# A fused linear-attention and gated-MLP kernel: q's features from narrow products spread by way of DRAM, low weight parts last in one block, all step orders replanned

## The chip, the cores and the metric

The kernel runs on one core of one Trainium2 chip. A core has TensorE (matrix products into PSUM), VectorE, ScalarE, GpSimd and SyncE, which run side by side and wait for one another by semaphores; SyncE issues the DMAs here. The metric is the device time of one execution in microseconds.

## The reference

Four batches, four heads of 32 features, 1088 positions. First a linear attention whose feature map is an outer product, then a gated MLP with a spatial product over the positions:

```
phi(x) = (S1 x) outer (S2 x)            # 8 x 8 = 64 features of each head
kv  = sum_s phi(k) v ;  z = sum_s phi(k)
x   = phi(q) kv / (phi(q) z + 1e-6)     # heads side by side: [4, 1088, 128]
h   = gelu(x @ w_in)                    # 1024 wide; u, v = its two halves
v_n = layernorm(v) * g_ln
v_s = w_sg @ v_n + b_sg                 # over the 1088 positions
out = x + (u * v_s) @ w_out
```

Everything is float32.

## The kernel before, in words

Positions lie in nine tiles of 128 (t; the last has 64) or in three thirds of 364, 362 and 362 columns (ci). The 512 wide hidden half is cut into four blocks of 128 (db).

Outside batch 0's first stretch every product is made of rounded parts (fp32r): a high part, and a low part that is the remainder, so that one f32 product is three of them: high x high, high x low, low x high. The spatial product (`Gate.spatial`, L326 to 336) adds these three for each t and ci, so a block is 3 x 26 products. Its weights' low parts, w_l, are made on VectorE in the head (`w_lo`, L919 to 925), one subtraction of 128x1088 for each t.

The **head** is batch 0's attention and its block 0, with f32 operands (L911: `pz<-w_f,vn`), built by the class Head. Its work is a set of steps with an engine, a length, a list of steps before it, and a tail; `Steps.order` (L509) plans them by due times that it reckons backwards (`far`), and the program is written out in that order. Loads are steps of SyncE's queue. v is normalised tile by tile: statistics, then a reciprocal root for a group of tiles (`GROUPS`; `norm`, L622, its last part on GpSimd, L634 to 645; for the third group VectorE does it all, L275 to 298), then ScalarE writes vn (L303).

Behind the head, `Gate.main` (L406) runs the blocks of each batch. In batch 0 it begins with block 1, all three thirds in one loop over t. Outside the head the order of issue isn't the order of the loops alone: what is ready goes first, within priorities (AHEAD), and in this block the whole first third is issued before the others. The next batch's attention is interleaved with it: the class Side gives each of its steps a time from a table of numbers, FIRST for batch 1 and LATER for the others, and `tick` issues what is due after each piece of spatial work.

In that attention (`Attention`, L123 to 240), k's features are a product with both factors' columns side by side (`k1`, L136), a copy and a multiplication (L143), summed with v into pkv (`k2`, L157). q's features go by six parts (third x half of the features). `load_q` loads q twice, `q1` makes a rounded copy on 64 partitions and its remainder on the others (L186, L187), and `q2` computes each of the two factors already spread to all features (L195, L196), copies one (L200), multiplies (L203), rounds (L206) and takes the remainder on GpSimd (L208):

```
for i in range(2):
    pp = bank(f"pab{self.b}_{j}_{i}")[:, :cw]
    mm(pp, lhsT=sab_h[:, i], rhs=self.qt[j][:, :cw], start=True, stop=False)
    mm(pp, lhsT=sab_l[:, i], rhs=self.qt[j][:, :cw], start=False, stop=True)
```

`q3` (L210) multiplies the features with kv (numerator and denominator, pnd) and divides (L231).

Of the kernel before, what the change touches and what calls it, by code (L numbers as in the profile page):

```python
# [18 lines left out]
P = 128  # L19
NT = 9  # L20
# [11 lines left out]
GROUPS = ((0, 3), (3, 3), (6, 3))  # L32
# [10 lines left out]
]  # L43
LATER = [
# [22 lines left out]
def tile_kernel(ctx: ExitStack, tc: tile.TileContext, qd, kd, vd, sd, wd, bd, wind, gd, woutd, identd, outd):  # L67
# [5 lines left out]
    cpool = ctx.enter_context(tc.tile_pool(name="const", bufs=1))  # L73
    psum = ctx.enter_context(tc.tile_pool(name="ps", bufs=3, space=PSUM))
# [17 lines left out]
    mask2 = const([P, 2], "mask2")  # L92
    mask4 = const([P, H], "mask4")
    for m, n in ((mask2, 2), (mask4, H)):
        V.memset(m, 0.0)
        for r in range(H):
            V.memset(m[32 * r : 32 * r + 32, r % n : r % n + 1], 1.0)

    mask = const([P, 64], "mask")
    G.memset(mask, 0.0)  # L100
    G.memset(mask[0:64, 0:32], 1.0)
    G.memset(mask[64:128, 32:64], 1.0)
# [3 lines left out]
    sk = const([P, 2, 64], "sk")  # L106
    G.memset(sk[:, 1], 0.0)
    sab_h = const([P, 2, P], "sab_h", F32R)
    sab_l = const([P, 2, P], "sab_l", F32R)
# [11 lines left out]
    for i in range(WARM):  # L121
        mm(bank("warm")[:64, :64], lhsT=mask, rhs=mask, start=True, stop=True)
    class Attention:  # L123
        def __init__(self, b, pool, x):
            self.b, self.pool, self.x = b, pool, x
            self.kp, self.q, self.qt, self.qp = {}, {}, {}, {}
# [7 lines left out]
        def k1(self, t):  # L134
            pk = bank(f"pk{self.b}_{t}")[:, :P]
            mm(pk, lhsT=self.k[:, P * t : P * t + P], rhs=sk.rearrange("p a c -> p (a c)"), start=True, stop=True)  # L136
            yield
            ab = pk[:, 0:64].rearrange("p (h x r) -> p h x r", h=H, x=2)
            kb = self.pool([P, H, R], "kb", f"kb{self.b}_{t}")
            A.copy(kb, ab[:, :, 1])  # L140
            yield
            self.kp[t] = kp = self.pool([P, H, R, R], "kp", f"kp{self.b}_{t}")
            V.tensor_tensor(  # L143
                kp,
                ab[:, :, 0].unsqueeze(3).broadcast_to([P, H, R, R]),
                kb.unsqueeze(2).broadcast_to([P, H, R, R]),
                op=ALU.mult,
            )

        def k2(self, t):  # L150
            kp = self.kp.pop(t).rearrange("p h i j -> p (h i j)")
# [23 lines left out]
        def load_q(self, j):  # L175
            ci, p = divmod(j, 2)
            c0, cw = CH[ci]
            self.q[j] = q = self.pool([P, CW], "qld", f"q{self.b}_{j}")
            for r in range(2):
                load(q[64 * r : 64 * r + 64, :cw], qd[self.b, 64 * p : 64 * p + 64, c0 : c0 + cw])  # L180

        def q1(self, j):
            q, cw = self.q.pop(j), CH[j // 2][1]

            self.qt[j] = qt = self.pool([P, CW], "qt", f"qt{self.b}_{j}", F32R)
            V.tensor_copy(qt[:, :cw], q[:, :cw])  # L186
            V.tensor_sub(qt[64:128, :cw], q[64:128, :cw], f32(qt[64:128, :cw]))  # L187

        def q2(self, j):
            ci, p = divmod(j, 2)  # L190
            cw = CH[ci][1]
            pab = []
            for i in range(2):
                pp = bank(f"pab{self.b}_{j}_{i}")[:, :cw]
                mm(pp, lhsT=sab_h[:, i], rhs=self.qt[j][:, :cw], start=True, stop=False)  # L195
                mm(pp, lhsT=sab_l[:, i], rhs=self.qt[j][:, :cw], start=False, stop=True)  # L196
                pab.append(pp)
            yield
            a = self.pool([P, 512], "r", f"a{self.b}_{j}")[:, :cw]
            A.copy(a, pab[0])  # L200
            yield
            qp = self.pool([P, 512], "r", f"qp{self.b}_{j}")[:, :cw]
            V.tensor_mul(qp, pab[1], a)  # L203
# [857 lines left out]
```

## Time and profile before

| | |
|---|---|
| time, median of 3 runs | 368.19 us (367.65 to 368.26) |
| profiled execution: its time | 367.63 us |
| profiled execution: span | 365.9 us |
| TensorE busy | 353.1 us, 97% |
| VectorE busy | 261.8 us, 72% |
| ScalarE busy | 163.8 us, 45% |
| GpSimd busy | 29.4 us, 8% |
| moved by DMA | 18.47 MB |
| granted TensorE clock, mean | 0.993 |

PE is TensorE, DVE VectorE, ACT ScalarE, POOL GpSimd, SP SyncE. The span runs from the first to the last instruction of the profiled execution, and a little of the execution's time lies around it. Matrix products overlap, so a row's duration is longer than the distance from its start to the next one's. The granted clock is TensorE's share of its full speed.

### The profile page before, as it was taken

What the parts mean: (1) busy time and instruction counts of PE and PEld (TensorE: products, weight loads), DVE (VectorE), ACT (ScalarE), POOL (GpSimd) and SP (SyncE); (2) the same over time, 40 slices, a digit from 0 to 9 for tenths busy, and PEclk for the clock granted to TensorE, in tenths of its full rate; (3) what the DMA queues carried; (4) which work ended last, traced back from release to release, by engine and by line L of the source; (5) the groups of instructions that cost most, each with busy time, mean ns of one, the idle gap of its engine ahead of it and who ended that gap; (6) DMA issues with size and microseconds to landing.
All of it is one profiled execution on the core that took longest, in us unless ns stands there. A gap on an engine that the chain in (4) does not pass through costs nothing.

```text
span 365.9 us, 5574 instructions
## 1 busy us (share of the span) xinstructions
PE 353.1 (97%) x2067; PEld 331.1 (91%) x2067; DVE 261.8 (72%) x626; ACT 163.8 (45%) x355; POOL 29.4 (8%) x60
## 2 busy tenths in 40 slices
PE   8995998999999999999999999999999999999995
PEld 8784657999988999999989999999999999999994
DVE  5786899889799775799897565698888453633234
ACT  5465951254463672445533931435533941331120
POOL 4006001010220000211200000202200000000000
PEclk9998999999999999999999999999999999999999
DMA  7992000150100000511000000100000000100001
GB/s 237 408 396 95 1 2 0 32 161 22 41 20 22 21 2 21 172 41 41 23 21 2 0 2 20 41 32 12 3 0 2 0 0 22 41 2 0 2 0 62
DMA packets 9772, 18.47 MB, mean 50 GB/s; under 512 B 1680, under 2 KB 6672, under 8 KB 9744
## 3 DMA queue, kind: packets, MB, share of 16 engines
q1 hardware_dynamic: 9744, 18.11, 14.5%
q8 instruction: 16, 0.26, 0.3%
q14 instruction: 12, 0.10, 0.1%
HBM read 15.88 MB, written 2.23 MB: 49 GB/s over the span
## 4 chain that ended last, share of the span: by engine, by line
PE 67%; DVE 11%; ACT 2%; issue 2%; DMA 1%; SPq 0%; DVEq 0%
PE pz L331 14%; PE pz L333 14%; PE pz L332 14%; PE pkv L157 3%; PE pu L345 2%; PE pu L347 2%; PE pu L346 2%; PE po L394 2%; PE po L395 2%; PE po L396 2%; PE pz L336 2%; PE pz L335 2%; PE pv L256 2%; PE pv L257 1%; PE pv L255 1%
## 5 line engine op out<-in xcount | busy, mean ns | idle before, releaser
L331 PE MATMUL pz<-w_h,vh 128*128 128x364 f32 (+1 forms) x360 | 119.5, 332 | 0.0
L333 PE MATMUL pz<-w_l,vh 128*128 128x364 f32 (+1 forms) x360 | 118.3, 328 | 0.7 <-DVE w_l L925 0.7
L332 PE MATMUL pz<-w_h,vl 128*128 128x364 f32 (+1 forms) x360 | 118.2, 328 | 0.0
L333 PEld LDWEIGHTS pz<-w_l,vh 128*128 128x128 f32 x360 | 67.6, 188 | 1.2 <-DVE w_l L925 1.0
L331 PEld LDWEIGHTS pz<-w_h,vh 128*128 128x128 f32 x360 | 67.8, 188 | 0.8 <-DVE gt L357 0.3
L332 PEld LDWEIGHTS pz<-w_h,vl 128*128 128x128 f32 x360 | 67.7, 188 | 0.7
L370 ACT CAST gh<-gt 128x362 fp32r<-128x362 f32 (+1 forms) x47 | 23.2, 495 | 86.2 <-PE po L395 80.2
L357 DVE SCALAR_TENSOR_TENSOR gt<-pz,g_col,b_bc 128x362 f32<-128x362 f32 (+1 forms) x48 | 28.0, 589 | 38.7 <-PE pz L336 38.3
L208 POOL TENSOR_TENSOR qpl<-qp,qph 128x362 fp32r<-128x362 f32 (+1 forms) x18 | 18.4, 1021 | 182.9 <-ACT kb L140 104.2
L303 ACT ACTIVATE vn<-vn,nm,rs 128x512 f32<-128x512 f32 x36 | 27.6, 809 | 10.0 <-DVE nm L298 7.3
L371 DVE TENSOR_TENSOR gl<-gt,gh 128x362 fp32r<-128x362 f32 (+1 forms) x47 | 25.8, 551 | 5.1 <-ACT gh L370 4.8
L321 DVE TENSOR_TENSOR vl<-vn,vh 128x384 fp32r<-128x384 f32 (+2 forms) x60 | 22.9, 419 | 8.2 <-ACT vh L316 8.1
L350 ACT ACTIVATE u<-pu 128x362 f32<-128x362 f32 (+1 forms) x48 | 22.4, 470 | 12.1 <-PE pu L347 11.8
L365 DVE TENSOR_TENSOR gt<-gt,u 128x362 f32<-128x362 f32 (+1 forms) x48 | 26.8, 560 | 0.4 <-ACT u L350 0.3
L227 DVE RECIPROCAL den<-den 128x362 f32<-128x362 f32 (+1 forms) x9 | 21.7, 2414 | 3.0 <-ACT den L224 2.9
L316 ACT CAST vh<-vn 128x384 fp32r<-128x384 f32 (+1 forms) x63 | 23.5, 419 | 0.9 <-PE pz L336 0.8
L911 PE MATMUL pz<-w_f,vn 128*128 128x362 f32 (+3 forms) x54 | 18.2, 489 | 4.0 <-ACT vn L303 4.0
L260 ACT ACTIVATE vn<-pv 128x512 f32<-128x512 f32 x27 | 15.7, 596 | 12.3 <-PE pv L257 12.2
L263 DVE BATCH_NORM_STATS2 st<-vn 128x6 f32<-128x512 f32 x27 | 18.3, 687 | 3.5 <-ACT vn L260 3.4
L911 PEld LDWEIGHTS pz<-w_f,vn 128*128 128x128 f32 (+1 forms) x54 | 10.1, 194 | 10.9 <-ACT vn L303 4.2
L345 PE MATMUL pu<-x_h,win_h 128*128 128x362 f32 (+1 forms) x48 | 16.7, 348 | 1.1 <-DVE x L231 0.7
L347 PE MATMUL pu<-x_l,win_h 128*128 128x362 f32 (+1 forms) x48 | 15.8, 329 | 0.0
(180 smaller groups left out, 602.9 us busy)
## 6 DMA issues: line engine op xcount, KB each, us to landing
w_f<-in_w SPq DMA_DIRECT2D x9, 544.0 KB, 9.0
vx<-in_v SPq DMA_DIRECT2D x8, 288.0 KB, 4.6
q<-in_q SPq DMA_DIRECT2D x24, 90.5 KB, 2.4
k<-in_k SPq DMA_DIRECT2D x3, 576.0 KB, 4.2
out<-o SPq DMA_DIRECT2D x8, 181.0 KB, 1.9
q<-in_q SPq DMA_DIRECT2D x12, 91.0 KB, 2.4
win_raw<-in_w_in SPq DMA_DIRECT2D x2, 512.0 KB, 7.1
out<-o SPq DMA_DIRECT2D x4, 182.0 KB, 1.8
```

Of the source, the lines that this page charges most:

```text
L303: A.activation(self.vn[:, t], self.vn[:, t], AF.Identity, bias=self.nm[:, t : t + 1], scale=self.rs[:, t : t + 1])
L316: A.copy(vh[:, ts], vs[:, ts])
L331: mm(z, lhsT=vh[:, t], rhs=w_h[:, t, cs], start=(t == 0), stop=False)
L332: mm(z, lhsT=vl[:, t], rhs=w_h[:, t, cs], start=False, stop=False)
L333: mm(z, lhsT=vh[:, t], rhs=w_l[t][:, cs], start=False, stop=False)
L345: mm(pu, lhsT=win_h[:, ws], rhs=xh[:, cs], start=True, stop=False)
L347: mm(pu, lhsT=win_h[:, ws], rhs=xl[:, cs], start=False, stop=True)
L357: V.scalar_tensor_tensor(gt, z, g_col[:, db : db + 1], b_bc[:, c0 : c0 + cw], op0=ALU.mult, op1=ALU.add)
L365: V.tensor_mul(gt, gt, u)
L370: A.copy(gh, gt)
L371: V.tensor_sub(gl, gt, f32(gh))
L911: return mm(zs[ci], lhsT=g.vn[r, t, :P], rhs=w_f[t][r, c0 : c0 + cw], start=(t == 0), stop=(t == NT - 1),)
```

## The change

1. q's features in batches 1 to 3. q is loaded once per third. The two factors are computed narrow, 64 wide, by one set of three products per third (`q2`), copied to SBUF, and spread to the features' partitions by three writes to a buffer in DRAM and two reads back (`spread`). The multiplication (`qp2`) then has both operands in SBUF. k's features are laid out in the same new order (`features`). The eight GpSimd steps that built sab_h and sab_l in the head fall away, and a mask comes with the identity's load.
2. Block 1 of batch 0: all high products first (`spatial_h`), then the 27 with the weights' low parts (`spatial_l`). The steps that make the low parts are due later in the head (tail −10).
3. The head is replanned: a table HEAD is added to the due times, the ends of the loads are modelled in sequence, GROUPS is (0,2)(2,3)(5,4) and only its second group has its norm on GpSimd; q1 and q2 are loaded ahead of v; one half of w_in is loaded behind all of w.
4. FIRST and LATER have new numbers.

```
-GROUPS = ((0, 3), (3, 3), (6, 3))
+GROUPS = ((0, 2), (2, 3), (5, 4))
...
 FIRST = [
-    -16.769, 0.232, -0.448, 2.644, -3.941, 2.17, -14.543, -2.337, 7.458, 11.494, 4.424, -3.889, 5.58, 19.523,
...
+    8.367, 12.087, 9.623, 6.432, 6.419, 24.648, 11.799, 24.091, 14.517, 39.473, 17.629, 25.126, 22.662, 41.732,
...
+    def spread(pool, ab, cw, name):
+        d = dram.tile([2, 2, P, 3 * P], F32, tag="e", name=name + "d", bufs=3)
+        load(
+            d[0].rearrange("p (x j) c -> (p x) j c", j=R)[:, :, :cw],
+            ab[:32, :cw].unsqueeze(1).broadcast_to([32, R, cw]),
+        )
+        for p in range(2):
+            load(
+                d[1, p].rearrange("(i x) c -> x i c", i=R)[:, :, :cw],
+                ab[32 + 16 * p : 48 + 16 * p, :cw].unsqueeze(1).broadcast_to([16, R, cw]),
+            )
+        e = [pool([P, 2, 3 * P], "e" + x, name + x) for x in "ab"]
+        for i in range(2):
+            load(e[i][:, :, :cw], d[i].rearrange("p q c -> q p c")[:, :, :cw])
+        return e
...
+        def q1(self, ci):
+            q, cw = self.q.pop(ci), CH[ci][1]
+            self.qt[ci] = qh, ql = [self.pool([P, CW], "qt", f"qt{self.b}_{ci}{i}", F32R) for i in "hl"]
+            A.copy(qh[:, :cw], q[:, :cw])
+            V.tensor_sub(ql[:, :cw], q[:, :cw], f32(qh[:, :cw]))
...
+            mm(pp, lhsT=sk_h, rhs=qh[:, :cw], start=True, stop=False)
+            mm(pp, lhsT=sk_l, rhs=qh[:, :cw], start=False, stop=False)
+            mm(pp, lhsT=sk_h, rhs=ql[:, :cw], start=False, stop=True)
+            ab = self.pool([64, 3 * P], "ab", f"ab{self.b}_{ci}")
+            A.copy(ab[:, :cw], pp[:64])
+            self.e[ci] = spread(self.pool, ab, cw, f"e{self.b}_{ci}")
+
+        def qp2(self, j):
...
+            a, b = (x[:, p, :cw] for x in self.e[ci])
+            V.tensor_mul(a, a, b)
...
-                for t in range(NT):
-                    if t in (3, 5, 7):
-                        run(self.split(2, 3 * (t // 2 - 1), 3))
+                for i in range(2 * NT):
+                    t = i % NT
+                    if i in (SPL):
+                        run(self.split(2, 3 * SPL.index(i), 3))
                     for ci in range(len(CH)):
-                        self.spatial(zs[ci], 1, ci, t)
+                        (self.spatial_l if i >= NT else self.spatial_h)(zs[ci], 1, ci, t)
...
-                if t0 < 6:
+                if t0 == 2:
                     self.norm(t0, n_)
...
-side = Pool(sp, 1, r=8, kp=3, kb=2, qld=1, qt=3, st=2, vh=2, vl=2, ve=3, y=3, h=3, p=3)
+side = Pool(sp, 1, r=6, kp=3, kb=2, qld=1, qt=3, ab=2, ea=2, eb=2, st=2, vh=2, vl=2, ve=3, y=3, h=3, p=3)
```

Three places of the new order. The first is TensorE around the first spatial product of the head; pv is x times w_in's v half, pz the spatial product, px a transpose of x. Before:

```order
L880 MATMUL pv0_5_427<-win_h_91,x0_h_131 128x512
L881 MATMUL pv0_5_427<-win_l_92,x0_h_131 128x512
L882 MATMUL pv0_5_427<-win_h_91,x0_l_132 128x512
L852 MATMUL px0_2_447<-ident_141,xt0_2_417 128x128 x3
L911 MATMUL pz0_0_0_467<-w_f0_204,vn0_133 128x364
L880 MATMUL pv0_7_484<-win_h_91,x0_h_131 128x512
L881 MATMUL pv0_7_484<-win_l_92,x0_h_131 128x512
```

And in the changed kernel:

```order
L913 MATMUL pv0_5_397<-win_h_84,x0_h_124 128x512
...
L820 MATMUL pab0_5_0_402<-q0_2_140,sab_144 128x384
L820 MATMUL pab0_5_1_404<-q0_2_140,sab_144 128x384
L944 MATMUL pz0_0_0_414<-w_f0_184,vn0_126 128x364
L944 MATMUL pz0_0_1_417<-w_f0_184,vn0_126 128x362
L944 MATMUL pz0_0_2_424<-w_f0_184,vn0_126 128x362
L859 MATMUL pnd0_2_443<-kvx_143,qp0_0_141 128x66
...
L944 MATMUL pz0_0_0_414<-w_f1_193,vn0_126 128x364
...
L885 MATMUL px0_2_463<-ident_73,xt0_2_457 128x128 x3
L944 MATMUL pz0_0_2_424<-w_f1_193,vn0_126 128x362
...
L913 MATMUL pv0_8_475<-win_h_84,x0_h_124 128x512
```

The third transpose and the last products of v now stand behind the first spatial products instead of ahead of them, and two tiles of vn are enough to begin.

The second place is TensorE in block 1 of batch 0 (vh, vl: the parts of v; w_h, w_l: of the weights; pab: q's factors). Before:

```order
L331 MATMUL pz0_1_0_638<-w_h_87,vh0_1_526 128x364
L332 MATMUL pz0_1_0_638<-w_h_87,vl0_1_527 128x364
L333 MATMUL pz0_1_0_638<-w_l7_606,vh0_1_526 128x364
L335 MATMUL pz0_1_0_638<-w_h_87,vh0_1_526 128x364
L136 MATMUL pk1_2_656<-sk_83,k1_628 128x128
L157 MATMUL pkv1_668<-vx_81,kp1_0_648 128x128 x2
L336 MATMUL pz0_1_0_638<-w_l8_608,vh0_1_526 128x364
L136 MATMUL pk1_1_662<-sk_83,k1_628 128x128
L331 MATMUL pz0_1_2_640<-w_h_87,vh0_1_526 128x362
L332 MATMUL pz0_1_2_640<-w_h_87,vl0_1_527 128x362
```

In the changed kernel, where the high products end and the low ones begin:

```order
L363 MATMUL pz0_1_0_618<-w_h_80,vh0_1_479 128x364
L363 MATMUL pz0_1_1_619<-w_h_80,vh0_1_479 128x362
L363 MATMUL pz0_1_2_620<-w_h_80,vh0_1_479 128x362
L226 MATMUL pab1_1_687<-qt1_1h_683,sk_h_78 128x362
L227 MATMUL pab1_1_687<-qt1_1h_683,sk_l_79 128x362
L371 MATMUL pz0_1_0_618<-w_l0_537,vh0_1_479 128x364
L178 MATMUL pk1_1_705<-sk_76,k1_608 128x128
...
L371 MATMUL pz0_1_0_618<-w_l1_574,vh0_1_479 128x364
...
L228 MATMUL pab1_1_687<-qt1_1l_684,sk_h_78 128x362
L371 MATMUL pz0_1_0_618<-w_l3_579,vh0_1_479 128x364
```

No product of the block takes a low weight part before all high ones are issued.

The third place is VectorE, where the low parts are made (kp: k's features; gt: a scaled spatial result; qt: q's remainder). Before:

```order
L925 TENSOR_TENSOR w_l3_594<-w_f3_232,w_h_87 128x1088
L321 TENSOR_TENSOR vl0_1_527<-vn0_133,vh0_1_526 128x384
L925 TENSOR_TENSOR w_l4_598<-w_f4_242,w_h_87 128x1088
L925 TENSOR_TENSOR w_l5_600<-w_f5_250,w_h_87 128x1088
L925 TENSOR_TENSOR w_l6_602<-w_f6_256,w_h_87 128x1088
L321 TENSOR_TENSOR vl0_1_527<-vn0_133,vh0_1_526 128x256
L324 TENSOR_TENSOR vh0_1_526<-vn0_133,vh0_1_526 64x128
L925 TENSOR_TENSOR w_l7_606<-w_f7_260,w_h_87 128x1088
L143 TENSOR_TENSOR kp1_0_648<-pk1_0_644,kb1_0_646 128x256
```

In the changed kernel:

```order
L958 TENSOR_TENSOR w_l2_576<-w_f2_198,w_h_80 128x1088
L666 TENSOR_TENSOR wout_l_87<-wot_551,woe_562 128x512
L958 TENSOR_TENSOR w_l3_579<-w_f3_208,w_h_80 128x1088
L392 SCALAR_TENSOR_TENSOR gt0_0_0_600<-pz0_0_0_414,g_col_88,b_bc_89 128x364
...
L958 TENSOR_TENSOR w_l4_581<-w_f4_216,w_h_80 128x1088
L141 TENSOR_TENSOR kp1_2_647<-pk1_2_643,kb1_2_645 128x256
L958 TENSOR_TENSOR w_l5_583<-w_f5_220,w_h_80 128x1088
L141 TENSOR_TENSOR kp1_0_661<-pk1_0_657,kb1_0_659 128x256
L958 TENSOR_TENSOR w_l6_585<-w_f6_225,w_h_80 128x1088
L220 TENSOR_TENSOR qt1_1l_684<-q1_1_681,qt1_1h_683 128x362
...
L141 TENSOR_TENSOR kp1_1_709<-pk1_1_705,kb1_1_707 128x256
L958 TENSOR_TENSOR w_l8_589<-w_f8_237,w_h_80 64x1088
```

The low parts are spread out between scalings, k features and q steps, which stand ahead of the last ones now.

## Rows read from the trace of the kernel before

**Rows 1.** the page: busy time of each engine; the chain of waits by engine

```profile
PE 353.1 (97%) x2067; PEld 331.1 (91%) x2067; DVE 261.8 (72%) x626; ACT 163.8 (45%) x355; POOL 29.4 (8%) x60
...
PE 67%; DVE 11%; ACT 2%; issue 2%; DMA 1%; SPq 0%; DVEq 0%
```

**Rows 2.** timeline of PE, 59 to 65: start us, us, what [idle before <-releaser]

```profile
60.12 0.43 PE L333 MATMUL pz<-w_l,vh 128*128 128x364 f32 x1 [0.72 <-DVE w_l L925]
...
61.73 0.41 PE L336 MATMUL pz<-w_l,vh 128*128 128x364 f32 x1 [0.34 <-DVE w_l L925]
62.58 0.49 PE L136 MATMUL pk<-sk,k 128*128 128x128 f32 x2 [0.44 <-DVE kp L143]
...
63.07 0.33 PE L332 MATMUL pz<-w_h,vl 128*128 128x362 f32 x1
...
64.89 0.49 PE L331 MATMUL pz<-w_h,vh 128*128 128x362 f32 x2
```

**Rows 3.** stretches: window, us, busy PE, PEld, DVE, ACT, POOL, clock, DMA, GB/s

```profile
10.00:15.00 5.00, 5.00 (x30) 3.81 (x29) 3.58 (x11) 1.19 (x3) 0.00 (x0) 1.00 1.02 413
30.00:35.00 5.00, 1.42 (x3) 0.88 (x4) 4.00 (x12) 2.28 (x4) 4.01 (x14) 0.81 0.03 12
63.00:150.00 87.00, 86.23 (x526) 81.86 (x525) 70.06 (x168) 41.75 (x100) 7.52 (x8) 1.00 0.15 43
150.00:360.00 210.00, 209.30 (x1259) 206.19 (x1257) 138.40 (x322) 87.74 (x192) 10.85 (x11) 1.00 0.06 18
```

**Rows 4.** timeline of PE, 28 to 54, columns as in rows 2

```profile
33.59 1.58 PE L911 MATMUL pz<-w_f,vn 128*128 128x364 f32 x2 [4.05 <-ACT vn L303]
...
36.59 0.39 PE L881 MATMUL pv<-win_l,x_h 128*128 128x512 f32 x1
...
39.58 14.77 PE L911 MATMUL pz<-w_f,vn 128*128 128x362 f32 x46
```

**Rows 5.** groups by line: count | busy us, mean ns | idle before <-releaser

```profile
L195 PE MATMUL pab<-qt,sab_h 128*128 128x362 f32 (+1 forms) x36 | 12.3, 342 | 0.0
...
L925 DVE TENSOR_TENSOR w_l<-w_f,w_h 128x1088 fp32r<-128x1088 f32 (+1 forms) x9 | 11.6, 1289 | 0.4
...
L187 DVE TENSOR_TENSOR qt<-q,qt 64x362 fp32r<-64x362 f32 (+1 forms) x18 | 10.3, 572 | 0.6
...
L186 DVE CAST qt<-q 128x362 fp32r<-128x362 f32 (+1 forms) x18 | 7.0, 389 | 6.5 <-DMA q<-in_q 4.5 <-PE pab L196 1.9
```

**Rows 6.** the page, DMA issues: count, KB each, us from issue to landing

```profile
w_f<-in_w SPq DMA_DIRECT2D x9, 544.0 KB, 9.0
...
k<-in_k SPq DMA_DIRECT2D x3, 576.0 KB, 4.2
out<-o SPq DMA_DIRECT2D x8, 181.0 KB, 1.9
```

**Rows 7.** timeline of POOL, the first group's norm: its first and last step

```profile
28.65 0.19 POOL L634 TENSOR_TENSOR nh<-ny 128x3 f32<-128x3 f32 x1 [21.77 <-DVE ny L631]
...
32.49 0.19 POOL L645 TENSOR_TENSOR nm<-np,rs 128x3 f32<-128x3 f32 x1
```

**Rows 8.** timeline of DVE: the last group's norm, then what follows to block 1

```profile
40.92 0.16 DVE L275 TENSOR_SCALAR ve<-mv 128x3 f32<-128x3 f32 x1
...
43.18 0.68 DVE L620 TENSOR_TENSOR win_l<-wi0t,wi0e 128x512 fp32r<-128x512 f32 x1
...
61.51 0.68 DVE L620 TENSOR_TENSOR wout_l<-wot,woe 128x512 fp32r<-128x512 f32 x1
```

**Rows 9.** views of lines 203 and 365: duration ns min/median/max, first and last start

```profile
L203 DVE TENSOR_TENSOR qp<-pab,a x18: 527/535/539, 71.5 to 260.4; 128x362 f32<-128x362 f32 x12, 128x364 f32<-128x364 f32 x6
...
L365 DVE TENSOR_TENSOR gt<-gt,u x48: 474/530/1306, 64.8 to 360.0; 128x362 f32<-128x362 f32 x32, 128x364 f32<-128x364 f32 x16
```

**Rows 10.** timelines of POOL and DVE at 165, columns as in rows 2

```profile
165.13 1.35 POOL L208 TENSOR_TENSOR qpl<-qp,qph 128x362 fp32r<-128x362 f32 x1 [0.40 <-ACT qph L206]
...
165.57 1.31 DVE L365 TENSOR_TENSOR gt<-gt,u 128x362 f32<-128x362 f32 x1
```

More of the change, by code (lines that the diff above doesn't have):

```diff
@@ L135, in k1 @@
             pk = bank(f"pk{self.b}_{t}")[:, :P]
[L136 removed]
+            mm(pk, lhsT=self.k[:, P * t : P * t + P], rhs=sk, start=True, stop=True)
             yield
[L138 to L140 removed]
+            kb = self.pool([P, 32], "kb", f"kb{self.b}_{t}")
+            A.copy(kb, pk[:, 32:64])
             yield
[L142 to L148, printed above, removed]
+            self.kp[t] = kp = self.pool([P, 2 * P], "kp", f"kp{self.b}_{t}")
+            features(kp, pk, kb)
         def k2(self, t):
[L151 removed]
+            kp = self.kp.pop(t)
             if t == 0:
@@ L173, in kv, with load_q @@
             V.tensor_sub(self.kvs[1], kv, f32(self.kvs[0]))
-        def load_q(self, j):
-            ci, p = divmod(j, 2)
+        def load_q(self, ci):
             c0, cw = CH[ci]
[L178 to L187, printed above, removed]
@@ L210, in q3 @@
+            G.tensor_sub(qpl, a, f32(qph))
         def q3(self, ci):
@@ L329, in spatial, with spatial_l @@
             cs = slice(c0, c0 + cw)
+            last = mm(z, lhsT=vh[:, t], rhs=w_h[:, t, cs], start=(t == 0), stop=False)
             if t < NT - 1:
-                mm(z, lhsT=vh[:, t], rhs=w_h[:, t, cs], start=(t == 0), stop=False)
-                mm(z, lhsT=vl[:, t], rhs=w_h[:, t, cs], start=False, stop=False)
-                mm(z, lhsT=vh[:, t], rhs=w_l[t][:, cs], start=False, stop=False)
-            else:
-                mm(z, lhsT=vh[:, t], rhs=w_h[:, t, cs], start=False, stop=False)
-                mm(z, lhsT=vh[:, t], rhs=w_l[t][:, cs], start=False, stop=True)
+                last = mm(z, lhsT=vl[:, t], rhs=w_h[:, t, cs], start=False, stop=False)
+            return last
+        def spatial_l(self, z, db, ci, t):
+            c0, cw = CH[ci]
+            mm(z, lhsT=self.parts[db][0][:, t], rhs=w_l[t][:, c0 : c0 + cw], start=False, stop=(t == NT - 1))
         def unit(self, pool, db, ci):
@@ L518, in far @@
                     s = steps[n]
-                    way[n] = s[1] + s[6] + max([far(u) for u in users[n]] + [s[7]])
+                    way[n] = s[1] + max(s[6], 0.0) + max([far(u) for u in users[n]] + [s[7]])
                 return way[n]
+            for n, more in zip(steps, HEAD):
+                far(n)
+                way[n] += more
             for n in steps:
                 far(n)
-            free, end, holds, given = {}, {}, {}, {}
+            free, end, holds, given, moved = {}, {}, {}, {}, 0.0
             left, out, rank = set(steps), [], {n: i for i, n in enumerate(steps)}
@@ L551, in order @@
                 free[eng] = t + length
-                end[n] = t + length + late
+                if late < 0:
+                    moved = max(moved, t + length + 1.5) - late / 360
+                    end[n] = moved + 0.4
+                else:
+                    end[n] = t + length + late
                 for b, tag, _ in takes:
@@ L575, in __init__, with load @@
             self.s = Steps()
-            self.dma = 0
-        def load(self, name, kb, f, after=(), queue="SP"):
-            self.dma += kb
-            self.s.at(name, queue, 0.47 if queue == "SP" else 0.1, f, after, late=2.0 + max(0.0, self.dma / 360 - 1.5))
+        def load(self, name, kb, f, after=()):
+            self.s.at(name, "SP", 0.47, f, after, late=-kb)
         def split64(self, name, hi, lo, raw, n, whole, after, late):
@@ new lines, in build, with expand @@
+            at("skh", "A", 0.2, lambda: A.copy(sk_h, sk), ["sk"], late=0.1, tail=-8)
+            at("skl", "V", 0.2, lambda: V.tensor_sub(sk_l, sk, f32(sk_h)), ["skh"], tail=-8)
+            sab = stage([P, 2, 2, P], "sab", "sab")
+            def expand(x, h):
+                part = s[:, R * x : R * x + R].unsqueeze(2 - x).broadcast_to([P, R, R])
+                o = sab[:, x, h // 2].rearrange("q (i h j) -> q h i j", i=R, h=2)[:, h % 2]
+                A.activation(o, part, AF.Copy, scale=mask4[:, h : h + 1])
@@ L732, in build @@
+            for h in range(H):
+                for x in range(2):
+                    at(("sab", x, h), "A", 0.25, lambda x=x, h=h: expand(x, h), [("s", "whole")])
             pk = {}
```

192 lines of the change are left out of this document (87 added, 105 removed), and 35 rows, old and new, of tables (FIRST, HEAD, LATER).

## The prediction

> **What bounds the kernel now.** I read the page first, then a table of stretches, then the idle times of the engine that turned out to matter. On the page TensorE is busy 353.1 of 365.9 us and holds two thirds of the chain that ended last; VectorE comes second with 261.8 [rows 1]. Most of TensorE's instructions behind the head are products of 362 or 364 columns, and they run back to back: between the start at 63.07 and that at 64.89 lie eleven of them, so one more or less costs 1.82 / 11 = 0.165 us, half of the 0.33 us that a row prints as its duration, since neighbours overlap [rows 2]. The stretches show where TensorE stands still. From 63 to 360 us it is idle 0.8 + 0.7 = 1.5 us in all; VectorE is busy 70.1 of the first 87 us there and 138.4 of the other 210 [rows 3]. So behind 63 us the kernel is as long as its list of products, and only fewer products can help. Before that TensorE stands twice. In batch 0's head it waits 4.05 us until 33.59, for ScalarE's normalised v (vn), and then runs at a lower clock: the granted clock from 30 to 35 is 0.81 on average, part of it at the lower level of 1.2 GHz after an idle engine, where the later stretches have 1.00 (2.4 GHz), and the six products that start from 33.59 on need 3.0 us to 36.59 where the same ones at the full clock take four at 0.23 and two at 0.30, 1.5 us. That stop costs 4.05 + 1.5 = 5.6 us [rows 3, 4]. In block 1 of batch 0 three products wait 0.72, 0.34 and 0.44 us for low weight parts and a k feature out of VectorE; from start to start they lose 0.88, 0.51 and 0.68, 2.1 us [rows 2].
>
> The sum below is made against the profiled execution: span 365.9, its own time 367.63, so 1.7 lie around the span. The median of the three runs, 368.19, is 0.56 above it.
>
> **q's features: −7.4.** For each of six parts of a batch and each of two factors a pair of products (L195 and L196, 36 of each in three batches, 72) [rows 5] gives way to three products per third, 27. Every one has 362 or 364 columns, so 45 x 0.165 = 7.4 us go from an engine without slack. VectorE loses 18 casts (7.0) and 18 subtractions (10.3) and gets 9 subtractions of the same length on twice the partitions (9 x 0.57 = 5.1); its 18 multiplications stay, but read two buffers in SBUF instead of PSUM and SBUF. That is 12 us less on an engine that isn't the bound, so nothing by itself. ScalarE swaps 18 copies for 9 casts and 9 copies of equal width: nothing, at 45% busy [rows 1]. GpSimd keeps its 18 subtractions.
>
> What the change adds is the way round DRAM: copy (0.5), three writes, two reads, multiplication (0.54), cast (0.5), GpSimd's subtraction (1.0). A write and a read are both 745 KB in two directions; the nearest rows for one such transfer are 1.9 us for 181 KB and 4.2 us for 576 KB [rows 6]. With some 0.5 us for each issue the chain lasts 0.5 + 1.5 + (1.9 to 4.2) + 1.0 + (1.9 to 4.2) + 0.5 + 0.5 + 1.0 = 9 to 13 us. I take 13, because every row goes to many partitions. In the new order at least 121 TensorE rows, 20 us, lie between a third's products and the first that reads its features. I cost it at nothing: what hides it are those 20 us. If that cover were gone, each third would stop TensorE by what is left of 13. SyncE's queue holds the reads behind the writes, and the next q, k and v loads behind the reads; these are taken up tens of us later, and the queue moved 43 GB/s in 63 to 150 where the early loads ran at 413 [rows 3]. In the queue the wait for the writes is thus long but bare.
>
> **The head: −1.8.** The norm of the first tiles moves from GpSimd to VectorE and covers two tiles instead of three. On GpSimd it lasted from 28.65 to 32.68 [rows 7], 4.0 us, behind VectorE's first three steps; the same twelve small steps on VectorE lasted from 40.92 to 43.18, 2.3 us [rows 8]. I stepped the new order by hand with the mean duration of each instruction. TensorE then runs out of work near 29.0 and gets the first spatial product at 30.3, so 1.3 us idle for 4.05, too short, I take it, to lose the clock. What is late next: v's second half has 384 KB of q1 and q2 put ahead of it, at 413 GB/s [rows 3] 0.9 us, and the products that take it wait for it; 0.35 before the first numerator; and 1.3 around the last third's transpose, since that third comes later and nothing is left to put before it. Together 0.9 + 0.35 + 1.3 + 1.3 = 3.85 new against 5.6 old: −1.8, and the f32 block ends near 52.5 instead of 54.3 [rows 4]. The bounds: −5.6 if none of these waits comes true, and +1.7 if they are half as long again (5.8) and one drops the clock as before (1.5). The value lies near the upper end, because the waits that go are replaced by waits of the same kind.
>
> **Low weight parts last: −1.3.** The block's 51 high products now run before its 27 low ones. TensorE begins them near 53, and reaches the last low one after 51 x 0.165 = 8.4, two small k products (0.4), six q products (1.0), 24 low ones (4.0) and three k products (0.7): 52.5 + 0.5 + 14.5 = 67.5. VectorE had 18.3 us of work from the end of its norm (43.18) to the last low part (61.51) [rows 8]. The new order puts into that stretch three steps of win (1.5), wout's low part (0.6), two k features (0.7), two q subtractions (1.0) and three scalings (1.5): 23.6. Its norm ends near 43.7, so the last part is there at 67.3. Nothing is left to wait for, with 0.2 to spare; a low part (1.29 on VectorE [rows 5]) more would already show. The 2.1 us go, and some 0.8 come back right behind, where the k features that were put off are waited for by their products until about 74. The bounds are −2.1 (nothing comes back) and +2.5 (VectorE two low parts late, 2.6, on top of what is there today).
>
> **The rest: +0.4.** Tables for batches 1 to 3 are new, and somewhere a product will stand. What is idle there today is 1.5 [rows 3], so −1.5 at best; +4 if the first stage's VectorE (81% busy) [rows 3] makes its consumers wait at a few places. I take a value near zero, since VectorE has 12 us less to do.
>
> **Sum:** −7.4 − 1.8 − 1.3 + 0.4 = −10.1: a span of 355.8, 357.5 for such an execution, **358.1** beside the median.
>
> **The rivals.**
> *Better (B).* The head's new waits don't come, nor those behind it. For it: each of my four waits is a difference of sums of mean durations and not longer than their error. Against it: v's second half really arrives later. −7.4 − 5.6 − 1.3 = −14.3, 353.9.
> *Part given back (C).* The stretch from 63 to 150 becomes bound by VectorE, and its share of the gain, 15 x 0.165 = 2.5, is lost; and the head's stop lasts long enough to lose the clock again, 1.5. For it: 81% busy there, with the scalings and k features pushed behind the low parts. Against it: 4 us less of q work per batch. −10.1 + 4.0 = −6.1, 362.1.
> *Slower (D).* GpSimd holds up VectorE. The 18 multiplications took 527 to 539 ns whatever else ran while one operand came from PSUM; the gate's multiplication, two operands in SBUF, took 530 mostly, but 1306 at most [rows 9], and that one, at 165.57, lies under GpSimd's subtraction of 165.13 [rows 10]. If all 18 go from the one kind to the other under such a subtraction, each gains 0.78 us, 14.0 us. They decide from the point where 13 of them lie on TensorE's path (13 x 0.78 = 10.1); with all, 372.1. Against it: the two multiplications of a third stand apart in the order, and a third's features have 7 us to spare. The Trainium skill, "SBUF — State Buffer", section "Who interferes with whom", states that a VectorE instruction with two inputs in SBUF contends with a GpSimd instruction that reads SBUF, and that the other blocks entirely; the two rows agree, 1306 against 530. By that rule alone the gain would be lost; by the slack it is not.
> *No change (E).* Each way through DRAM takes what the loads of w took, 9.0 us for 544 KB [rows 6]. The chain is then 0.5 + 1.5 + 9.0 + 1.0 + 9.0 + 2.0 = 23 us against 20, and each of the tightest thirds, one per batch, stops TensorE 3 us: 9 us in three batches, 367.1, and with the clock lost once more 368.6. It decides only from a transfer of 7.5 us on. Against it: the loads of w queued at 413 GB/s behind one another, and the later stretch moves a tenth of that.
>
> **How the numbers follow.** My forecast has 0.62, B 0.15, C 0.16, D 0.04, E 0.03. The range reaches from B to C with what the bounds of the head and of the rest add, 353.5 to 363.5; D and E and the far ends stay outside. A measurement of this kernel can tell about 0.2% from no change. Forecast, B and C lie on the fast side by more: 0.93; E is within: 0.03; D slower: 0.04.
>
> **What would show it.** The changed profile should have 27 products for q's narrow factors in place of the 72; TensorE busy near 345; one stop of 1 to 2 us before the first spatial product, with a granted clock near 1.00 from 30 to 35; no wait for low weight parts; from 63 to 360 under 3 us idle; the multiplications of the q features partly at 1.3 us. I am wrong in the main if TensorE is idle over 5 us behind 63 us, if a numerator's product waits for q's features, or if the head still loses its clock.

## The result, and the profile after

The changed kernel takes 363.17 us (median of 4 runs, 362.88 to 363.34) against 367.93 for the kernel before; the ratio is 0.987 (95% interval 0.9852 to 0.9887), 4.8 us less. The forecast was 358.1, in a range from 353.5 to 363.5: the sign was right, the median lies just inside the range, and the gain is less than half of the 10.1 us that the sum had. The profiled execution took 363.20, its span is 361.4.

The page of the changed kernel, busy time and chain, as in [rows 1]:

```profile
PE 350.6 (97%) x2022; PEld 321.6 (89%) x2022; DVE 249.3 (69%) x603; ACT 162.4 (45%) x355; POOL 22.0 (6%) x37
...
PE 81%; DVE 9%; ACT 5%; DMA 1%; issue 1%; SPq 1%; POOL 1%; DVEq 0%; ACTq 0%
```

The 45 products are gone, and VectorE is down by the 12 us that were reckoned. TensorE is "97% busy" as it was, but its busy time fell by 2.5 us only. The stretches of the changed kernel, columns as in [rows 3]:

```profile
30.00:35.00 5.00, 4.84 (x24) 3.48 (x25) 4.20 (x14) 3.66 (x6) 2.66 (x12) 1.00 0.04 14
63.00:150.00 87.00, 85.60 (x517) 80.05 (x517) 69.52 (x158) 43.61 (x107) 7.01 (x7) 1.00 0.41 109
150.00:355.00 205.00, 204.53 (x1203) 196.64 (x1201) 126.98 (x305) 83.11 (x184) 11.58 (x12) 1.00 0.18 47
```

The head keeps its clock (1.00 for 0.81). Behind 63 us TensorE is idle 1.4 + 0.5 = 1.9 us, hardly more than before. Its timeline shows the waits in the head and one behind block 1, as in [rows 2, 4]:

```profile
8.43 0.46 PE L788 MATMUL pkv<-vx,vn 128*128 128x128 f32 x2 [0.69 <-DMA vx<-in_v]
9.08 3.17 PE L788 MATMUL pkv<-vx,vn 128*128 128x128 f32 x26 [0.18 <-DMA vx<-in_v]
...
30.16 2.10 PE L944 MATMUL pz<-w_f,vn 128*128 128x364 f32 x6 [1.23 <-ACT vn L335]
...
37.32 0.50 PE L913 MATMUL pv<-win_h,x_h 128*128 128x512 f32 x1 [0.19 <-ACT x_h L888]
...
44.88 7.78 PE L944 MATMUL pz<-w_f,vn 128*128 128x364 f32 x24 [0.19 <-ACT vn L335]
...
69.15 0.60 PE L193 MATMUL pkv<-vx,kp 128*128 128x128 f32 x3 [0.35 <-DVE gt L392]
```

Where the time went is seen by stages. I take a batch's start as the start of the first spatial product of its block 0, and count products in the trace. A stage's length comes from one profiled execution; in two runs of near copies of the changed kernel its third line is 230.10 and 229.80:

| stage | before | changed | difference | forecast |
|---|---|---|---|---|
| head, to its last f32 product | 53.88 | 52.20 | −1.7 | −1.8 |
| batch 0, from block 1 on | 73.28 | 69.82 | −3.5 | −2.5 − 1.3 |
| batches 1 to 3, to the last spatial product | 230.48 | 230.41 | −0.1 | −5.0 + 0.4 |
| from there to the end | 7.22 | 7.97 | +0.8 | 0 |

(The head's line has times on the span's clock, the others have lengths; block 1 starts 1.00 behind the head's last product in both.) The third line's ends are these products, of the kernel before and of the changed one:

```profile
128.16 0.33 PE L331 MATMUL pz<-w_h,vh 128*128 128x364 f32 x1
...
358.64 0.33 PE L336 MATMUL pz<-w_l,vh 128*128 128x362 f32 x1
```

```profile
123.02 0.33 PE L363 MATMUL pz<-w_h,vh 128*128 128x364 f32 x1
...
353.43 0.32 PE L371 MATMUL pz<-w_l,vh 128*128 128x362 f32 x1
```

Thirty of the 45 products lay between them, 30 x 0.165 = 5.0 us, and nothing is left of these. Idle time of PE doesn't show why, but that of the weight loads (PEld) does, which run ahead of the products (the load for the product at 353.43 starts at 353.26). What the weight loads waited for, kernel before, 128 to 359 us (us in total, times, longest; waits under 0.15 us are not counted):

```profile
PEld pu L345 <- issue: 1.1, 1, 1.1
PEld pu L345 <- DVE kp L143: 0.4, 1, 0.4
PEld pz L331 <- DVE gt L357: 0.3, 2, 0.2
PEld pv L255 <- ACT vn L260: 0.2, 1, 0.2
```

The changed kernel, 122.9 to 354 us, the first six of eleven lines:

```profile
PEld pv L287 <- ACT vn L292: 1.1, 5, 0.3
PEld pnd L252 <- POOL qpl L240: 0.9, 4, 0.3
PEld pz L363 <- DVE gt L392: 0.8, 3, 0.4
PEld pu L380 <- ACT u L385: 0.7, 2, 0.5
PEld pv L287 <- ACT u L385: 0.6, 3, 0.2
PEld pz L363 <- ACT vh L348: 0.6, 2, 0.4
```

Five waits and 2.0 us became 26 and 6.3 us, none longer than 0.5 and behind many producers: vn, q's remainder, scalings, u, vh. The products say the same when they are counted by the distance between the starts of neighbours, less the median distance of a pair of these two widths in both kernels. What is more than 0.04 us over the median I call a stop: 29 stops with 3.5 us became 72 with 7.8 us. The medians alone add up to 4.9 us less, which is the worth of the 30 products. So the products went at the price reckoned, and the stops took most of it back. The Trainium skill, "Trainium Kernel Development and Optimization", section "Performance Expectations", says that the busy time of products is a bad metric for how close a kernel is to its limit, since they are pipelined, and the busy share of the weight loads a good one; these traces agree, PE stays at 97% and PEld falls from 91% to 89%.

### The profile page after: what moved, and what is told of

Read it like the earlier page. It is cut to its first block, busy times and chain, and to the rows that moved or that the text cites. A ratio compares the mean times of both kernels' runs of the same rounds, so it can differ in the third digit from the quotient of the medians.

```text
span 361.4 us, 5443 instructions
## 1 busy us (share of the span) xinstructions
PE 350.6 (97%) x2022; PEld 321.6 (89%) x2022; DVE 249.3 (69%) x603; ACT 162.4 (45%) x355; POOL 22.0 (6%) x37
## 4 chain that ended last, share of the span: by engine, by line
PE 81%; DVE 9%; ACT 5%; DMA 1%; issue 1%; SPq 1%; POOL 1%; DVEq 0%; ACTq 0%
PE pz L363 18%; PE pz L371 17%; PE pz L365 16%; PE pkv L193 3%; ACT vn L335 2%; PE pz L944 2%; PE pv L287 2%; PE pu L380 2%; PE po L431 2%; PE pk L178 2%; PE po L430 2%; PE po L429 2%; PE pv L288 1%; PE pv L289 1%; PE pu L382 1%; PE pu L381 1%
## 5 line engine op out<-in xcount | busy, mean ns | idle before, releaser
L363 PE MATMUL pz<-w_h,vh 128*128 128x362 f32 (+1 forms) x405 | 134.1, 333 | 0.2
L371 PE MATMUL pz<-w_l,vh 128*128 128x362 f32 (+1 forms) x405 | 129.6, 329 | 0.0
L363 PEld LDWEIGHTS pz<-w_h,vh 128*128 128x128 f32 x405 | 76.0, 188 | 1.9 <-DVE gt L392 0.8
L371 PEld LDWEIGHTS pz<-w_l,vh 128*128 128x128 f32 x405 | 75.5, 188 | 0.3
L400 DVE TENSOR_TENSOR gt<-gt,u 128x362 f32<-128x362 f32 (+1 forms) x48 | 25.7, 541 | 3.2 <-ACT u L385 2.9
L406 DVE TENSOR_TENSOR gl<-gt,gh 128x362 fp32r<-128x362 f32 (+1 forms) x47 | 24.6, 529 | 2.4 <-ACT gh L405 1.8
L141 DVE TENSOR_TENSOR kp<-pk,kb 128x256 f32<-128x256 f32 x27 | 11.2, 421 | 7.8 <-ACT kb L181 5.6
L431 PE MATMUL po<-gl,wout_h 128*128 128x362 f32 (+1 forms) x47 | 15.8, 336 | 0.9 <-DVE gl L406 0.9
## 6 DMA issues: line engine op xcount, KB each, us to landing
w_f<-in_w SPq DMA_DIRECT2D x9, 544.0 KB, 10.5
```

The lines of the kernel that those rows point to most:

```text
L363: last = mm(z, lhsT=vh[:, t], rhs=w_h[:, t, cs], start=(t == 0), stop=False)
L371: mm(z, lhsT=self.parts[db][0][:, t], rhs=w_l[t][:, c0 : c0 + cw], start=False, stop=(t == NT - 1))
L400: V.tensor_mul(gt, gt, u)
L406: V.tensor_sub(gl, gt, f32(gh))
L431: mm(o, lhsT=wout_h[:, db], rhs=gl, start=False, stop=(db == NB - 1))
```

## The experiments

My theories after the result: (1) the new tables put consumers right behind their producers; (2) the way round DRAM costs time, because it makes a third's features late (2b: not by waits for it, but by moving a batch's attention as a whole); (3) every product is a little slower. Three other runs test the head, the block and GpSimd. The engines' orders outside the head are laid out when the kernel is built, by lengths reckoned for each step, so most edits move other rows too.

**Part 2 alone.** The kernel before, with `spatial_h`, `spatial_l`, the loop over both and the tail −10 of the low parts:

```
-                    for ci in range(len(CH)):
-                        self.spatial(zs[ci], 1, ci, t)
+                    for ci in range(len(CH)):
+                        (self.spatial_l if i >= NT else self.spatial_h)(zs[ci], 1, ci, t)
```

> The kernel before with part 2 of the change alone: block 1 of batch 0 takes its high products first, its 27 low ones last, and the low parts are due later. If the prediction's term for this block holds, the stops of 2.1 us behind low parts go and some 0.8 come back: 1.3 us less than before, 366.6. Rival: VectorE's work put off behind the low parts is waited for further on, and nothing is left of it by the end of batch 0: 367.9, with three stops of 0.3 us or more between 65 and 85 us instead of those between 59 and 63.

369.82 against 368.32, ratio 1.0038 (1.0025 to 1.005): slower by some 1.5 us. Its timeline of TensorE:

```profile
71.84 1.60 PE L159 MATMUL pkv<-vx,kp 128*128 128x128 f32 x12 [0.59 <-DVE kp L145]
74.47 0.49 PE L138 MATMUL pk<-sk,k 128*128 128x128 f32 x2 [0.57 <-DVE kp L145]
79.95 0.43 PE L333 MATMUL pz<-w_h,vh 128*128 128x364 f32 x1 [0.29 <-DVE kv L169]
83.55 0.44 PE L221 MATMUL pnd<-qph,kv_l 128*128 128x364 f32 x1 [0.44 <-DVE kv_l L175]
```

The stops behind low parts are gone and block 1 is 2.3 us shorter, but batch 0 from block 1 on is 1.5 longer in all, with stops behind late k features: the rival. The head, in another order, is 1.0 longer in the profiled execution, which is the slowest of the six. By itself part 2 wins nothing; in the changed kernel it comes with k steps planned later and less q work.

**The old places.** The changed kernel, both tables filled from those of before; of LATER, three of the entries:

```
-    k1 of t=0: -2.62    first multiplication: 18.816    last numerators: 65.059
+    k1 of t=0: 3.718    first multiplication: 21.226    last numerators: 64.054
```

> The changed kernel with the steps of the interleaved attention at the times that they have in the tables of before (the narrow products 22 units ahead of where the wide ones stood, the multiplications where they stood). Theory 1, the new places put consumers right behind their producers: TensorE's weight loads wait some 2 us in all behind 123 us instead of 6, and the time falls by 3 to 4 us to 359 to 360. Theory 2, the way round DRAM makes the features late: nothing is won, 363, or more, since that way is as long as in the changed kernel. Theory 3, every product is a little slower (0.1660 us from start to start against 0.1655): 363 as well, with the same step.

382.77 (ratio 1.0398, 1.0353 to 1.0443). Theory 1 in its plain form falls: the old places are far worse. Weight loads now wait 8.3 us for q's remainder, in 14 waits, and 8.4 for vh: at the old places the numerators stand right behind the steps that make their operands. In batch 0 the multiplications stand right behind the reads too (reads of two thirds land at 85.1 and 99.2, the multiplications start at 85.2 and 99.7). So the old places can't tell the order from the way.

**Two products for three.**

```
-            mm(pp, lhsT=sk_l, rhs=qh[:, :cw], start=False, stop=False)
```

> The changed kernel without the product of the rounded q with the low part of the factors' weights: two products per third instead of three, 9 fewer, so q's factors lack that part. Theory 1, 0.165 us is the price of a product where TensorE sets the pace: 9 x 0.165 = 1.5 us less, 361.7. Rival: in the batches with an interleaved attention the producers set the pace and products are free there: 363.2, the waits of the weight loads longer by 1.5 us.

362.99 (ratio 0.9851, 0.9835 to 0.9866; the changed kernel's is 0.987): 0.7 us of the 1.5 by the ratios, 0.2 by the times, not clear of the noise. In batches 1 to 3, which lost 6 products, the stage lasts 230.83 for 230.41. The rival holds there: in these batches of the changed kernel a product less is worth nothing, and the stops grow from 7.8 to 9.3 us.

**The reads twice.**

```
-            load(e[i][:, :, :cw], d[i].rearrange("p q c -> q p c")[:, :, :cw])
+            for _ in range(2):
+                load(e[i][:, :, :cw], d[i].rearrange("p q c -> q p c")[:, :, :cw])
```

> The changed kernel with both reads of each third issued twice: 6.7 MB more from DRAM, the way of the features 4 us longer. Theory 1: features land 7 to 18 us ahead of their multiplication, so the time stays within 0.6 us of 363.2. Theory 2, the way is on the path: at least 3 of 9 thirds come 4 us later for the products that read them, 12 us, and even half of that gives 369.

378.84 (ratio 1.0289, 1.0255 to 1.0323). Theory 1's expectation is missed by 15 us. Numerators wait 4.0 us in all, for q's remainder; most of the waiting is at the end of each batch's attention. It isn't the longer transfer that the multiplications wait for: the reads of the last third of batch 1 land at 179.9, and its multiplication starts at 199.2. So it is rather the order laid out around a longer read that costs the time. Weight loads, 54 to 370 us:

```profile
PEld pz L364 <- ACT vh L349: 7.2, 6, 3.7
PEld pv L288 <- ACT x_h L268: 4.4, 2, 3.1
PEld pnd L253 <- POOL qpl L241: 4.0, 6, 0.8
```

**No way round DRAM.** Reads of the same size, from q's rows:

```
-            load(e[i][:, :, :cw], d[i].rearrange("p q c -> q p c")[:, :, :cw])
+            load(e[i][:, :, :cw], qd[0:2].rearrange("p q c -> q p c")[:, :, :cw])
```

> The changed kernel, its reads of each third taken from q's own rows in DRAM instead of the buffer that the three writes fill, so they wait for no write (the features of q are then wrong; writes, reads and all later work keep their sizes). Theory 2b, the length of the way round DRAM puts q's features, and with them the whole rest of a batch's attention, late in the batch, where it is squeezed: the first numerator of batches 2 and 3 comes some 26 us after the batch's first product instead of 34, as in the kernel before, the short waits behind 123 us fall from 6 to 2 or 3, and the time falls by 2 to 4, to 359 to 361. Theory 1, the tables alone put consumers too close: 363 within 0.7.

362.22 (ratio 0.9848, 0.9831 to 0.9864), only 1 us less in all, but by stages: batches 1 to 3 last 228.12 for 230.41, and batch 0 1.4 us longer, by its own changed order. The last numerators' products of batch 1, in the kernel before, the changed one and this one:

```profile
181.93 0.32 PE L220 MATMUL pnd<-qpl,kv_h 128*128 128x362 f32 x1
```

```profile
187.72 0.43 PE L252 MATMUL pnd<-qpl,kv_h 128*128 128x362 f32 x1
```

```profile
176.52 0.33 PE L252 MATMUL pnd<-qpl,kv_h 128*128 128x362 f32 x1
```

From the batch's start (128.16, 123.02, 123.89) these are 53.8, 64.7 and 52.6 us. The first numerators didn't come earlier as expected (34 us), but the last ones by 12, and 2.3 us of the batches' time went with them: 0.3 of it are three products that stand in batch 0 in this order, 1.8 are stops (7.8 to 6.0), and the waits of the weight loads fall from 26 to 12. But the run takes away more than the way. Its features need neither the writes nor the products in front of them, and the multiplications move far ahead: those that the changed kernel has in batches 1 and 2 now stand before these batches begin, ahead of the products whose results they would have taken. The last third's, in the changed kernel and in this one (duration ns, first and last start):

```profile
L237 DVE TENSOR_TENSOR e_2a<-e_2a,e_2b x6: 503/528/531, 105.8 to 270.5; 128x362 f32<-128x362 f32 x6
```

```profile
L237 DVE TENSOR_TENSOR e_2a<-e_2a,e_2b x6: 518/528/535, 82.4 to 195.0; 128x362 f32<-128x362 f32 x6
```

The run so shows what the whole chain of q's features costs in these batches, some 2 us of the 5, and not the way's share of it.

**Features first.**

```
-            V.tensor_mul(a, a, b)
-            A.copy(qph, a)
-            G.tensor_sub(qpl, a, f32(qph))
+            with tc.high_priority(AHEAD):
+                V.tensor_mul(a, a, b)
+                A.copy(qph, a)
+                G.tensor_sub(qpl, a, f32(qph))
```

> The changed kernel with the multiplication, the rounding and the remainder of q's features at high priority, so that each engine's order has them as early as their data are reckoned to be there; only 16 rows of TensorE move. Theory 1, their low priority makes numerators wait: the 0.9 us of waits for GpSimd's remainder go, 362.3. Theory 2b, they are as early as their data allow already: 363.2 within 0.6.

362.77 (ratio 0.9861, 0.9845 to 0.9878), not to be told from the changed kernel; the waits for the remainder stay. The multiplications stay where they were (those of the last third in batch 1 start 61.5 us into it, for 61.6), so it isn't their priority that puts them there.

**The remainder on VectorE.**

```
-            G.tensor_sub(qpl, a, f32(qph))
+            V.tensor_sub(qpl, a, f32(qph))
```

> The changed kernel with the remainder of q's features on VectorE (0.53 us where GpSimd takes 0.97). If GpSimd's length and its hold on VectorE's second operand cost the path: waits for the remainder (0.9 us behind 123 us) halve, no multiplication takes 1.3 us, 362.5. Rival, VectorE has no room for 18 x 0.53 = 9.5 us more: waits of TensorE for VectorE grow, 364 to 366.

365.05 (ratio 0.9922, 0.9907 to 0.9937), some 1.9 slower than the changed kernel, as the rival had it: VectorE had no room, block 3 of batch 0 lost 3.3 us.

**Multiplications planned earlier.** All 12 entries of the multiplications in the two tables less 6; the last two of FIRST:

```
-    49.157, 71.241,
+    43.157, 65.241,
```

> The changed kernel with the 18 multiplications' times in both tables 6 units (some 4.7 us) earlier, nothing else touched. Theory 1: the times of the tables set when the features come, the first numerators of batches 2 and 3 come up to 4 us earlier, waits shrink by 1 to 2 us, 361.5 to 362.5. Theory 2b: their data's way sets it, so the times change little: 363.2 within 0.7, unless what is issued in their place stands worse.

389.23 (ratio 1.0595, 1.0559 to 1.0631), 26 us slower, which neither theory expected. In batch 0's block 3 and from there on the numerators came later, not earlier (the last of batch 1 at 209.3), and weight loads waited:

```profile
PEld pz L362 <- ACT vh L347: 9.6, 6, 4.4
PEld po L430 <- DVE gl L405: 4.0, 5, 2.0
PEld pv L286 <- ACT x_h L266: 2.9, 1, 2.9
```

In batch 1 six units put the last third's first multiplication (190.1) ahead of the last numerators of the third before (198.0). That this is a matter of the buffers they share is a guess that no run tests.

**Products taken from the kernel before.** 18 of L196's 36:

```
-                mm(pp, lhsT=sab_l[:, i], rhs=self.qt[j][:, :cw], start=False, stop=True)
+                if i:
+                    mm(pp, lhsT=sab_l[:, i], rhs=self.qt[j][:, :cw], start=False, stop=True)
```

> The kernel before without the low weight part of the first of q's two factors: 18 products fewer (of L196's 36), so that factor lacks this part. Theory A, TensorE sets the pace of the kernel before: 18 x 0.165 = 3.0 us less, 364.9, with as few short waits of the weight loads behind 128 us as before (2 us). Theory B, already there a product taken away is half swallowed by the producers: 366 or more, and the waits grow by 1.5 us.

366.36 against 368.16 (ratio 0.9939, 0.9919 to 0.9958): 1.8 for 3.0, between the two. By stages it is clear: batches 1 to 3, 12 products fewer, last 228.54 for 230.48, 1.94 us for 12 x 0.165 = 1.98. Batch 0 gives nothing for its six, 73.29 for 73.28, and the head, in another order, 0.65 longer. So the price of 0.165 was right in the later batches of the kernel before, and wrong in batch 0. The chain of waits that ended last says so too: of its time TensorE holds 97% in batches 1 to 3, but 31% in batch 0 from block 1 on, where VectorE holds 47%.

**No way round DRAM, and two products.** The two edits together.

> The kernel with reads that wait for no write, and two products of q's factors per third instead of three (q's features are wrong, and the low weight part is missing). Against the same kernel with three products (362.2): if it was the way round DRAM that swallowed the worth of a product in the changed kernel, all 9 x 0.165 = 1.5 us come, 360.7; if the producers' own chain sets the pace, less than 0.8, 361.5 or more.

362.92 (ratio 0.9856, 0.9831 to 0.9881): no gain over 362.2 in all. The whole time thus speaks for the producers. Batches 1 to 3 last 226.89 for 228.12, 1.2 us, but the new order also moved five other products out of them into batch 0, which is 1.5 longer. All eleven are worth 1.6 us by their distances, the five 0.6 of it; so the six that were dropped brought 0.6 of their 1.0, where they brought nothing with the way in place (230.83 for 230.41). Stages of near copies differ by 0.6 as well, so this doesn't decide between the two.

**Reads on GpSimd's queue.**

```
-            load(e[i][:, :, :cw], d[i].rearrange("p q c -> q p c")[:, :, :cw])
+            G.dma_start(e[i][:, :, :cw], d[i].rearrange("p q c -> q p c")[:, :, :cw])
```

> The changed kernel with the two reads of each third issued by GpSimd instead of SyncE, so that they stand behind no store that waits for its output (7 us of hold at 146 in the changed kernel) and the next third's writes stand behind no read. Theory 2b with the queue as a part of the way: features land up to 9 us earlier in batch 2, 362 to 363. Rival, the engines' orders are laid out around the lengths reckoned for SyncE, and any other ones cost more than the way gives: 366 or more.

368.50 (ratio 1.0001, 0.9985 to 1.0016), as slow as the kernel before, 5.3 us lost against the changed kernel: the time of the rival. Its cause isn't told apart from another one, for GpSimd is busy some 0.73 us with each of the 18 reads, and the weight loads' waits for its remainder grow from 0.9 to 2.4 us. The run also speaks against late numerators as the whole cause: the last ones of batches 1 and 2 come 62 us into the batch for 65, and batches 1 to 3 last 232.7 for 230.4. Of the kernels that leave nothing out, none beat the changed one clearly.

**The head's first norm on GpSimd.** HEAD's numbers stay with their steps; the one step more has none.

```
-                if t0 == 2:
+                if t0 < 5:
                     self.norm(t0, n_)
```

> The changed kernel with the norm of the head's first group back on GpSimd (its first three steps stay on VectorE, as in the kernel before); two tiles, and everything else planned as it is. The prediction's term for the head rests on 2.3 us of norm on VectorE against 4.0 on GpSimd. If it holds, the first spatial product of the head starts 1.7 to 2.3 us later than at 30.2, and the kernel takes 364.9 to 365.5, or up to 367 if TensorE's granted clock drops below 1.00 again between 30 and 35. Rival: with two tiles only, the start is set by ScalarE's writing of vn or by the weights, and the engine of the norm is nothing: 363.2 within 0.6.

364.33 (ratio 0.9908, 0.9892 to 0.9925), 1.2 slower; the head's last f32 product is 2.6 later. Timeline of TensorE:

```profile
29.63 3.93 PE L944 MATMUL pz<-w_f,vn 128*128 128x364 f32 x12 [1.05 <-ACT vn L335]
33.40 0.81 PE L820 MATMUL pab<-q,sab 128*128 128x384 f32 x2
34.86 0.88 PE L944 MATMUL pz<-w_f,vn 128*128 128x364 f32 x2 [0.65 <-ACT vn L335]
...
47.45 7.78 PE L944 MATMUL pz<-w_f,vn 128*128 128x364 f32 x24 [2.02 <-ACT vn L335]
```

The norm's engine, with the order that comes with it, counts, though not as I had it: the first product isn't late (a q product was moved behind it), and the time goes in later stops, the longest 2.02 us for 0.19 in the changed kernel.

## Why the prediction was right or wrong, point by point

- **What bounds the kernel: half right.** TensorE did set the pace of batches 1 to 3 before (1.94 of 1.98 us). But I read its slack from its idle time, 1.5 us [rows 3], where the starts of the products hold 3.5 us of stops from batch 1 on alone. And the price of 0.165 didn't hold in batch 0, where VectorE held more of the chain than TensorE. In the changed kernel TensorE holds 94% of the chain in batch 0 from block 1 on, and in batches 1 to 3 only 88%.
- **The head, −1.8: right in size, in its working by half**, −1.7 measured. v's second half was waited for 0.69 + 0.18 us (0.9 said), the first spatial product 1.23 (1.3 said), and the clock stayed at 1.00. The other two waits, 0.35 at the first numerator and 1.3 around the last third's transpose, did not come as such: behind 31 us TensorE stands 0.19 us twice. Smaller stops, the first of them among the k products, took their place, so that the sum fits better than its terms; that much was luck.
- **Low parts last, −1.3: right for the changed kernel, not by itself.** No product waits for a low part:

```profile
L371 PE MATMUL pz<-w_l,vh 128*128 128x362 f32 (+1 forms) x405 | 129.6, 329 | 0.0
```

  Batch 0 is 3.5 shorter for the 3.8 of this term and 15 products. Alone, the same edit made the kernel slower, so how much of the 3.5 is its own isn't shown.
- **q's features, −7.4, with the way round DRAM "at nothing": the step that failed.** The term took 45 x 0.165 in full, because "behind 63 us the kernel is as long as its list of products", and asked of the way only whether a numerator would stand waiting for it. In batches 1 to 3 the 30 products there, 5.0 us, brought 0.1. Their price was right (the distances without stops fell by 4.9 us); what failed is that the rest of the order would stay without gaps. The stops grew from 3.5 to 7.8 us, and six products fewer then shortened these batches by nothing.

  The way was longer than said: from the end of a third's copy to the landing of its last read it took 10.5 to 21.0 us, where the sum had 1.5 + 4.2 + 1.0 + 4.2 = 10.9. In batch 1 the first third's took 16.2, to 146.7, held up in SyncE's queue behind a store and the next third's writes:

```profile
130.81 0.56 SPq L151 DMA_DIRECT2D e_0d<-ab  x1
131.41 1.24 SPq L156 DMA_DIRECT2D e_0d<-ab  x2
136.03 0.38 SPq L162 DMA_DIRECT2D e_0a<-e_0d  x1
140.78 0.36 SPq L439 DMA_DIRECT2D out<-o  x1
141.24 0.56 SPq L151 DMA_DIRECT2D e_1d<-ab  x1
142.33 0.38 SPq L162 DMA_DIRECT2D e_0b<-e_0d  x1
```

  But its length isn't what the multiplications wait for. They stand in VectorE's order 2 to 22 us behind the landing of their reads; the last third's reads of batch 1 land at 166.6, its multiplication starts 18 us later, and VectorE wasn't idle before it:

```profile
161.53 0.36 SPq L162 DMA_DIRECT2D e_2b<-e_2d  x1
...
184.62 0.95 DVE L237 TENSOR_TENSOR e_2a<-e_2a,e_2b 128x362 f32<-128x362 f32 x2
```

  So the laid out order sets the place. In it the last numerators come 65 us into a batch instead of 54, and what is behind them (v, its norm, vh) has 11 us less before the next batch needs it. That this makes the short stops fits the run without the way and goes against the reads on GpSimd's queue, where they came earlier and the stops were 10.2 us. Where the stops come from is thus shown for some 2 us, the chain of q's features as a whole, and stays open for the rest.
- **The rest, +0.4: mis-sized.** It is where the bill came: +4.5 over the forecast in batches 1 to 3, so 4.9 in its place, beyond the end of +4 that I had given it. Of this, some 2 us go when q's features wait for nothing. Some 0.6, all that was seen of theory 3, may be no effect at all: a block of batch 3 with nothing beside it lasted 15.93 here and 15.90 before, and one run of a near copy of the changed kernel had 15.90 again and 229.80 for the stage. The remaining 2.3 us of short waits stay open.
- **After the last product**, +0.8 that no term had: 7.3 to 8.1 in the runs of kernels near to it. The engines' rows there are the same as before, so it is in the last store's landing or what follows it; open.
- **The rivals.** The time lies near C's (362.1), but not by its mechanism: neither was batch 0's share of the gain lost, nor the head's clock. D's mechanism exists, but only 2 of 18 multiplications met GpSimd, 1.6 us on VectorE at most, the longest shown here:

```profile
L237 DVE TENSOR_TENSOR e_1a<-e_1a,e_1b x6: 527/536/1334, 83.2 to 253.4; 128x362 f32<-128x362 f32 x6
```

  E named the way round DRAM, but by another mechanism: no third stopped TensorE by 3 us. The chances gave 0.62 to a sum whose largest term had been priced without its side effect.
- **The signs.** 27 products, the clock and no wait for low parts came as said, and TensorE's idle time behind 63 us stayed under 3. "TensorE busy near 345" did not: 350.6. And one of the signs of being wrong was there, small: numerators' weight loads waited 0.9 us in four waits for q's remainder.

## What to carry to other kernels

Taking products from a busy engine pays in full only while nothing else in the stage falls out of step; that no first reader waits for a detour doesn't show that the detour, and the order laid out around it, is free. Ask where the last step of the chain will then stand. Read slack from the starts of the products and from the waits of the weight loads; here an engine that is 97% busy lost 4 us more in stops too short to show as idle. Read the chain of waits by stages too: 67% for TensorE over the whole kernel before was 97% in the later batches and 31% in batch 0. Where an order is laid out ahead from reckoned lengths, a longer or shorter transfer changes the order, so an experiment that "takes out" one step moves others: look where they went before naming a cause. And judge an edit by stages, with the products of each counted, since one stage's luck can hide another's result.

## What the runs showed that I had not expected

Small edits to such a plan can cost several times the gain: 6 units on 12 table entries took 26 us, reads issued twice 15.7, the reads on another queue 5.3 (each against 363.17). And taking work away didn't shorten the kernel wherever the engine was "97% busy": 9 products gave 0.2 to 0.7 us, and with the way round DRAM taken out as well, nothing in all.
